# Every third PSUM copy of transposed p moves from ScalarE to VectorE, in the first batch

## The chip, the cores and the metric

The kernel runs on one core of one Trainium2 chip. Its engines, TensorE (PE, with its weight loads as PEld), VectorE (DVE), ScalarE (ACT), GpSimd (POOL) and SyncE (SP, which here issues the DMAs), each run their own list of instructions in order and wait for one another by semaphores. The metric is the device time of one execution in microseconds, the median of three runs.

## The reference

```python
def _attn_ref(q, k, v):                       # q, k, v: 4 x 8 x 1152 x 64, fp32
    q_pool = q.reshape(B, H, S // factor, factor, D).mean(axis=3)     # factor 2
    scores = scale * np.matmul(q_pool, k.transpose(0, 1, 3, 2))
    scores = scores - np.max(scores, axis=-1, keepdims=True)
    attn = np.exp(scores)
    attn = attn / (np.sum(attn, axis=-1, keepdims=True) + 1e-09)
    return np.matmul(attn, v).astype(np.float32)
...
    x = _moe_ref(x=x, **moe_kwargs)           # 512 -> 2048 -> 512, leaky relu
    return _moe2_ref(x=x, **moe2_kwargs)      # max of three 512 -> 768, then 768 -> 512
```

Attention over 4 batches of 8 heads, with each two rows of q averaged (576 queries against 1152 keys of 64), and behind it two MoE layers on the 2304 resulting rows.

## The kernel before

**Pairs and phases.** Heads are taken two at a time: 16 pairs, counted from 0, of which n = 0 to 3 are the first batch (NP = 4). The queries of a pair are worked in two phases: five tiles of 128 rows in the first (two of each head, and a fifth, `m`, of both), four in the second. A tile's scores are 128 x 1152 in three parts of 384. Nothing of the MoE layers can run until a batch's attention is through; from the second batch on MoE products and attention are interleaved, and TensorE always has MoE work to fill in. The first batch has none.

**A tile.** `scores` multiplies q by k (each split in two roundings) into three PSUM banks. In the first batch the outer two are a double bank, of which there are two (`s20`, `s21`), and the third is the single bank `s1`, used by every tile. VectorE takes the maximum of the double bank (L324, 128 x 768) and of the single one (L325, 128 x 384) and combines them (L326); ScalarE then takes the exponential of the single bank (L327), which frees it for the next tile's scores, and of the double one (L330). `normalise` (L348 to L354) makes the sums and, for the fifth tile, scales p.

**Transposes.** A phase has nine slots, one for each 128 keys. `probs_t` transposes that part of the phase's first four tiles on TensorE into one PSUM bank (`pst`, 128 x 512), and one copy (L377, on ScalarE) takes it to SBUF. Three such copies make a group (g = 0, 1, 2), `probs_m` adds the fifth tile's part for a group in a single copy (`psf`, L384, on VectorE), and `values` then multiplies the group with v into `pv`; `evac` takes the finished `pv` out (L422 to L424).

**What else uses the banks and the engines.** The pool `ps_m` has two banks in rotation, and everything else of the first batch goes through them: `psq` and `psk`, the transposes of q and k for the next pair, `pst`, `psf`, and `psr`, the sums. A bank is free again only when its copies are done: for `psq` scalings on ScalarE (L255), and their remainder on VectorE (L259); for `psk` two casts on ScalarE (L220) and two subtractions on VectorE (L223). The same engines also decode weights ahead of time: a load (L580), a scaling on ScalarE (L589) and a shift and a combination on VectorE (L592, L595), a rounding (L610), its remainder on GpSimd (L611), and a store (L619). Tiles of names `pspare`, `pend`, `kspare` and `qspare` are buffers lent by later parts.

**Order.** The program gives each slot its work in code, with preparation put at fixed slots. A scheduler then sets each engine's list, so an instruction's engine can change what stands near it. `EARLY` puts the maxima and exponentials ahead of work that the code issued some 300 instructions before them.

Of the kernel before, what the change touches and what calls it, by code (L numbers as in the profile page):

```python
# [22 lines left out]
def kernel(  # L23
# [21 lines left out]
    nc = tc.nc  # L45
    B, H, S, D = q.shape
    T = S // 2
    NP = H // 2
# [72 lines left out]
    def transpose(out, in_, eye):  # L121
        return on_pe(nc.tensor.transpose, out, in_, eye)
# [7 lines left out]
    def bank(name):  # L130
        turn[0] += 1
        pool = ps_w["m"] if ps_w and turn[0] % 2 == 0 else ps_m
        return pool.tile([128, 512], F32, tag="m", name=name)
# [154 lines left out]
    def keys_of(p, kt):  # L288
        c, k0 = divmod(kt * 128, SN)
        if c == 2:  # L290
            return p[1][:, k0:k0 + 128]
        return p[0].rearrange("p a b -> p (a b)")[:, kt * 128:(kt + 1) * 128]
# [75 lines left out]
    def probs_t(n, ph, kt):  # L368
        g = kt % PG
        if g == 0:  # L370
            pts[kt // PG] = pt_p.tile([128, PG, 2 * X0], F32, tag="pt", name="pt")
        w = (X0, T - X0)[ph]
        ps = bank("pst")
        for i in range(4):
            transpose(ps[:, i * 128:(i + 1) * 128], keys_of(ptl[n, ph, i], kt), ident)
        dst = pts[kt // PG][:, g, 0:2 * w].rearrange("p (j c) -> p j c", j=2)[:, :, 0:256]
        nc.scalar.copy(out=dst, in_=ps.rearrange("p (j c) -> p j c", j=2))  # L377

    def probs_m(n, gr):
        ps = bank("psf")  # L380
# [62 lines left out]
    def attention():  # L443
# [74 lines left out]
        for s in range(len(phases) * KT):  # L518
            n, ph = phases[s // KT]
            gr, g = divmod(s % KT, PG)  # L520
            done = 0
            want = CHAIN
            if s == 2 * NP * KT:
                done += yield from follow()
            probs_t(n, ph, gr * PG + g)
            done += TR * 4
            if g == PG - 1 and ph == 0:
                probs_m(n, gr)
                done += TR * PG
                want -= TR * PG  # L530
            c = now(s)
            if g == 0 and late:
                c += yield from follow()
            done += c
            yield done, max(0, want - c)
            yield 0, None
            if g == PG - 1:
                late.append((n, ph, gr))
# [133 lines left out]
    class Main:  # L672
        n = TM
# [11 lines left out]
    class Rest:  # L685
        n = TR_
# [102 lines left out]
    if True:  # L789
        nc.gpsimd.memset(ident, 0.0)  # L790
        nc.gpsimd.affine_select(
            out=ident, in_=ident, pattern=[[-1, 128]], compare_op=ALU.not_equal, fill=1.0, base=0, channel_multiplier=1
# [72 lines left out]
```

## Time and profile before

| what | value |
|---|---|
| median of 3 runs | 1360.38 us (1357.13 to 1360.44) |
| the profiled execution | 1356.42 us, of which its span 1354.7 us |
| TensorE busy | 1259.0 us, 93% |
| VectorE busy | 627.9 us, 46% |
| ScalarE busy | 633.5 us, 47% |
| GpSimd busy | 292.1 us, 22% |
| L377 copies of transposed p | 288, 167.4 us in all |
| first batch's attention | from about 33 us to 220 us |

The span is one profiled execution, seen from the first to the last instruction; 1.7 us of that execution lie outside. Busy shares are means over stages with different limits: the first fifth of the span, where the change lies, has gaps on every engine, and TensorE is nearly full behind it.

### The profile page before, as it was taken

How to read it: one execution, taken by the hardware profiler on the slowest of the kernel's cores; microseconds unless marked ns; L12 is line 12 of the kernel's file. 1: busy time of each engine (PE TensorE's matmuls, PEld its weight loads, DVE VectorE, ACT ScalarE, POOL GpSimd, SP SyncE). 2: the span in 40 equal slices, each digit the busy share in tenths (PEclk: the TensorE clock that was granted, in tenths of full speed). 3: DMA queues.
4: the chain of work that ended last, by engine and by line, in shares of the span. 5: the costliest groups of instructions: out<-in, count | busy, mean ns of one | idle time of the engine just before them, and what ended most of it. 6: DMA issues, size and time to landing. Idle time of an engine off the chain costs nothing.

```text
span 1354.7 us, 19162 instructions
## 1 busy us (share of the span) xinstructions
PE 1259.0 (93%) x7376; PEld 1015.6 (75%) x7376; DVE 627.9 (46%) x1106; ACT 633.5 (47%) x1253; POOL 292.1 (22%) x265
## 2 busy tenths in 40 slices
PE   5788878899898989999999989999999999999998
PEld 4556646677676877777787878787877788888888
DVE  5655554556656563455555454545464401222110
ACT  5767665666566664544444344545454422112111
POOL 1111022344454330121121010111110002224110
PEclk8888989999999999999999999999999999999999
DMA  5422053666767663444435344535343244333333
GB/s 158 123 74 57 18 149 118 215 210 209 248 202 229 208 188 131 132 136 131 154 126 157 123 128 163 149 109 150 128 141 116 95 154 154 129 126 124 108 126 109
DMA packets 86902, 193.29 MB, mean 143 GB/s; under 512 B 11292, under 2 KB 41756, under 8 KB 86812
## 3 DMA queue, kind: packets, MB, share of 16 engines
q1 hardware_dynamic: 86812, 192.08, 45.1%
q8 instruction: 58, 0.95, 0.3%
q14 instruction: 32, 0.26, 0.1%
HBM read 146.80 MB, written 35.13 MB: 134 GB/s over the span
## 4 chain that ended last, share of the span: by engine, by line
PE 75%; DMA 9%; DVE 7%; ACT 4%; issue 3%; POOL 2%; DVEq 0%; SPq 0%; ACTq 0%; POOLq 0%
PE m L108 41%; PE pv L108 10%; PE s L108 10%; PE pst L108 6%; PE o L108 6%; DMA wraw<-in_moe_w_out_dram 3%; DMA wraw<-in_moe_w_in_dram 2%; DMA wraw<-in_moe_w_dram 2%; DMA qraw<-in_q_dram 2%; DVE mx L334 1%; DVE wmant L595 1%; DVE mx L324 1%; ACT pt L377 1%; DVE q L259 1%; POOL wsplit L611 1%
## 5 line engine op out<-in xcount | busy, mean ns | idle before, releaser
L108 PE MATMUL m<-x,w 128*128 128x512 f32 x1224 | 308.9, 397 | 0.0
L108 PEld LDWEIGHTS m<-x,w 128*128 128x128 f32 x1224 | 222.7, 188 | 54.0 <-issue 12.8
L377 ACT COPY pt<-pst 128x512 f32<-128x512 f32 x288 | 167.4, 587 | 183.5 <-PE pst L108 182.3
L108 PE MATMUL s<-kt,q 128*128 128x384 f32 x840 | 190.6, 358 | 26.8 <-ACT p L335 14.1
L334 DVE TENSOR_REDUCE mx<-s 128x1 f32<-128x1152 f32 x108 | 146.4, 1355 | 116.2 <-PE s L108 114.9
L108 PEld LDWEIGHTS s<-kt,q 128*128 128x128 f32 x840 | 148.2, 195 | 39.2 <-ACT p L335 16.8
L108 PE MATMUL pst<-ident,p 128*128 128x128 f32 x1080 | 169.4, 277 | 8.4 <-ACT pt L377 3.5
L335 ACT ACTIVATE p<-s,mx 128x1152 f32<-128x1152 f32 x108 | 132.4, 1226 | 83.0 <-DVE mx L334 82.3
L108 PEld LDWEIGHTS pst<-ident,p 128*128 128x128 f32 x1080 | 131.6, 141 | 45.1 <-issue 11.6
L732 POOL TENSOR_TENSOR g<-t,g 128x512 fp32r<-128x512 f32 x64 | 84.5, 1322 | 369.7 <-DVE g L731 355.1
L108 PE MATMUL pv<-pt,v 128*64 128x320 f32 (+1 forms) x1008 | 149.9, 435 | 14.0 <-DVE pt L384 13.4
L108 PE MATMUL m<-g,w 128*128 128x512 f32 x576 | 149.8, 399 | 0.0
L108 PEld LDWEIGHTS m<-g,w 128*128 128x128 f32 x576 | 103.6, 188 | 24.5 <-issue 6.2
L108 PEld LDWEIGHTS pv<-pt,v 128*64 128x64 f32 x1008 | 67.8, 143 | 70.0 <-issue 20.5
L108 PE MATMUL m<-x,wsplit 128*128 128x512 f32 x408 | 108.5, 405 | 1.0 <-DVE kt L223 0.8
L730 ACT ACTIVATE t<-m 128x512 f32<-128x512 f32 x80 | 44.3, 555 | 128.2 <-PE m L108 128.2
L611 POOL TENSOR_TENSOR wsplit<-wmant,wsplit 128x512 fp32r<-128x512 f32 x56 | 74.1, 1327 | 92.8 <-ACT wsplit L610 71.0
L108 PEld LDWEIGHTS m<-x,wsplit 128*128 128x128 f32 x408 | 74.7, 191 | 20.5 <-issue 5.1
L731 DVE CAST g<-t 128x512 fp32r<-128x512 f32 x64 | 28.7, 448 | 111.2 <-ACT t L730 110.7
L760 DVE TENSOR_TENSOR t<-m,t 128x512 f32<-128x512 f32 (+1 forms) x60 | 38.2, 637 | 84.9 <-PE m L108 73.8
L670 POOL TENSOR_TENSOR y<-t,y 128x512 fp32r<-128x512 f32 x24 | 31.7, 1319 | 199.1 <-ACT y L669 199.1
L354 DVE TENSOR_SCALAR p<-p,sums 128x1152 f32<-128x1152 f32 x76 | 66.2, 870 | 2.7
(106 smaller groups left out, 1467.7 us busy)
## 6 DMA issues: line engine op xcount, KB each, us to landing
w<-w SPq DMA_DIRECT2D x168, 512.0 KB, 3.5
w<-wsplit SPq DMA_DIRECT2D x56, 512.0 KB, 5.1
wraw<-in_moe_w_out_dram SPq DMA_DIRECT2D x22, 512.0 KB, 4.1
wraw<-in_moe_w_dram SPq DMA_DIRECT2D x18, 512.0 KB, 4.0
qraw<-in_q_dram SPq DMA_DIRECT2D x15, 576.0 KB
kraw<-in_k_dram SPq DMA_DIRECT2D x15, 576.0 KB, 6.9
q<-q SPq DMA_DIRECT2D x52, 160.0 KB, 4.5
wraw<-in_moe_w_in_dram SPq DMA_DIRECT2D x16, 512.0 KB, 5.7
```

Source lines behind the costliest of these rows:

```text
L108: mm = f(*args, **kwargs)
L259: nc.vector.scalar_tensor_tensor(out=lo, in0=src, scalar=scale, in1=hi, op0=ALU.mult, op1=ALU.subtract)
L334: nc.vector.tensor_reduce(out=mx[:, 0:1], in_=ps[:, :, 0:SN], axis=AX.XY, op=ALU.max, negate=True)
L335: nc.scalar.activation(out=p[2], in_=ps[:, :, 0:SN], func=ACTF.Exp, bias=mx[:, 0:1], accum_out=rs[:, i:i + 1])
L354: nc.vector.tensor_scalar(out=x, in0=x, scalar1=rs[:, i:i + 1], scalar2=None, op0=ALU.mult)
L377: nc.scalar.copy(out=dst, in_=ps.rearrange("p (j c) -> p j c", j=2))
L611: nc.gpsimd.tensor_tensor(out=t[:, 1], in0=r, in1=t[:, 0], op=ALU.subtract)
L670: nc.gpsimd.tensor_tensor(out=t[:, 1], in0=src, in1=t[:, 0], op=ALU.subtract)
L730: nc.scalar.activation(out=t, in_=ps[:, 0:k.n], func=ACTF.Prelu, alpha=0.01)
L731: nc.vector.tensor_copy(out=gt[:, 0], in_=t)
L732: nc.gpsimd.tensor_tensor(out=gt[:, 1], in0=t, in1=gt[:, 0], op=ALU.subtract)
L760: nc.vector.tensor_tensor(out=t, in0=ps[:, 0:k.n], in1=t, op=ALU.max)
```

## The change

In the first batch the copy of the middle transposes of each group (g = 1; key parts 1, 4 and 7 of the nine) is issued on VectorE. That is 24 of the 288 copies. The bank, its size and its destination stay the same. Line numbers behind the edit are one higher in the changed kernel (L593 there is L592 here).

```diff
         dst = pts[kt // PG][:, g, 0:2 * w].rearrange("p (j c) -> p j c", j=2)[:, :, 0:256]
-        nc.scalar.copy(out=dst, in_=ps.rearrange("p (j c) -> p j c", j=2))
+        copy = nc.vector.tensor_copy if n < NP and g == 1 else nc.scalar.copy
+        copy(out=dst, in_=ps.rearrange("p (j c) -> p j c", j=2))
```

The scheduler puts other instructions of the first batch in a new order too; behind the first batch each engine's list is as it was, but for two neighbours on SyncE. Three places follow, as the difference of the lists (- before, + changed).

VectorE in the last group of pair 0's second phase; `mx_801` and `mx_832` are the maxima of the next phase's first two tiles, `pst_789` the middle transposes:

```order
 L324 TENSOR_REDUCE mx_801<-s20_117 128x1
 L325 TENSOR_REDUCE mx_801<-s1_119 128x1
+L378 COPY pt_767<-pst_789 128x512
 L324 TENSOR_REDUCE mx_832<-s21_118 128x1
 L326 TENSOR_REDUCE mx_801<-mx_801 128x1
```

The copy stands ahead of a second tile's maximum and of the combination for the first tile.

VectorE in the preparation of pair 3, in pair 1's second phase (`pst_1081` the middle transposes, `psk_1112` the first transposes of k):

```order
 L324 TENSOR_REDUCE mx_1099<-s20_117 128x1
+L378 COPY pt_1049<-pst_1081 128x512
 L325 TENSOR_REDUCE mx_1099<-s1_119 128x1
 L326 TENSOR_REDUCE mx_1099<-mx_1099 128x1
-L223 TENSOR_TENSOR kspare_317<-psk_1112,kspare_317 64x512 x2
 L348 TENSOR_TENSOR sums_941<-sums_941 128x5
 L349 TENSOR_SCALAR sums_941<-sums_941 128x5
 L350 RECIPROCAL sums_941<-sums_941 128x5
+L223 TENSOR_TENSOR kspare_317<-psk_1112,kspare_317 64x512 x2
```

The copy stands inside a tile's three maxima, and the subtractions for k have gone behind three steps on the sums. ScalarE at the same place:

```order
-L377 COPY pt_1049<-pst_1081 128x512
 L364 COPY rb256_122<-psr_1108 128x256
-L220 CAST kspare_317<-psk_1112 64x512 x2
+L220 CAST kspare_317<-psk_1112 64x512
 L327 ACTIVATE pend_1043,sums_941<-s1_119,mx_1099 128x384
 L330 ACTIVATE pspare_1100,sums_941<-s20_117,mx_1099 128x768
-L377 COPY pt_1049<-pst_1121 128x512
+L220 CAST kspare_317<-psk_1112 64x512
+L378 COPY pt_1049<-pst_1121 128x512
```

Between the two casts of k there now stands a tile's exponential.

VectorE at the end of pair 3's first phase (`wraw_2012` and `wraw_2075` are two weight loads one after the other, `pst_1684` the middle transposes, `mx_1751` the maximum of a tile of the next phase):

```order
-L595 SCALAR_TENSOR_TENSOR wmant_1940<-wraw_1938 128x512
+L596 SCALAR_TENSOR_TENSOR wmant_1940<-wraw_1938 128x512
+L596 SCALAR_TENSOR_TENSOR wmant_1950<-wraw_1948 128x512
 L223 TENSOR_TENSOR kt0_1642<-psk_1669,kt0_1642 64x512 x2
-L595 SCALAR_TENSOR_TENSOR wmant_1950<-wraw_1948 128x512
+L593 TENSOR_SCALAR wraw_2012<-wraw_2012 128x512
+L378 COPY pt_1662<-pst_1684 128x2x256
 L334 TENSOR_REDUCE mx_1751<-s_1741 128x1
```

The decode of `wraw_2012`, which waits for its load, has come ahead of the copy and of a maximum. A few instructions later on the same engine:

```order
-L592 TENSOR_SCALAR wraw_2012<-wraw_2012 128x512
-L384 COPY pt_1662<-psf_1714 128x6x64
-L595 SCALAR_TENSOR_TENSOR wmant_1978<-wraw_1976 128x512
+L593 TENSOR_SCALAR wraw_2075<-wraw_2075 128x512
+L385 COPY pt_1662<-psf_1714 128x6x64
+L596 SCALAR_TENSOR_TENSOR wmant_1978<-wraw_1976 128x512
 L223 TENSOR_TENSOR kt1_1643<-psk_1719,kt1_1643 64x512 x2
-L592 TENSOR_SCALAR wraw_2075<-wraw_2075 128x512
```

The decode of `wraw_2075` has come ahead of the fifth tile's copy. Its load has moved on SyncE, ahead of the load of the next batch's q:

```order
+L620 DMA w1_132<-wsplit_1934 128x1024
+L581 DMA wraw_2075<-in_moe_w_out_dram 128x4x256
 L171 DMA qraw_1838<-in_q_dram 72x2x1024
-L580 DMA wraw_2075<-in_moe_w_out_dram 128x4x256
-L264 DMA q10_125<-q10_125 64x640
```

The load follows directly on a store of split weights now.

## Rows read from the trace of the kernel before

**Rows 1.** Windows: each engine's busy us (instructions), clock, DMA share, GB/s.
```profile
33.00:185.00 152.00, 122.32 (x772) 88.29 (x773) 87.97 (x192) 106.00 (x251) 19.47 (x22) 0.93 0.24 63
...
220.00:1354.00 1134.00, 1091.26 (x6373) 894.57 (x6372) 503.77 (x848) 488.62 (x923) 260.06 (x218) 0.99 0.48 152
```

**Rows 2.** The chain that ended last, 33 to 185 us, by line.
```profile
by line: PE pv L108 20.0%; PE s L108 17.7%; PE pst L108 10.2%; DVE mx L324 7.9%; ACT pt L377 4.3%; issue 3.4%; DVE mx L325 2.9%; DVE kspare L223 2.9%; DMA wraw<-in_moe_w_in_dram 2.6%; ACT pspare L330 2.3%; DMA wraw<-in_moe_w_out_dram 2.3%; 
```

**Rows 3.** Waits of PE, 33 to 185 us: total us, times, longest.
```profile
PE psk L108 <- ACT pt L377: 4.0, 2, 2.3
PE pst L108 <- ACT pt L377: 3.5, 6, 1.6
```

**Rows 4.** Groups by form, DVE 33:220, ACT 33:185: busy, mean ns | idle before, releaser.
```profile
L324 DVE TENSOR_REDUCE mx<-s 128x1 f32<-128x768 f32 x31 | 29.6, 955 | 30.8 <-PE s L108 30.4
L325 DVE TENSOR_REDUCE mx<-s 128x1 f32<-128x384 f32 x31 | 17.1, 552 | 11.3 <-PE s L108 11.2
...
L384 DVE COPY pt<-psf 128x384 f32<-128x384 f32 x12 | 6.6, 549 | 0.0
...
L377 ACT COPY pt<-pst 128x512 f32<-128x512 f32 x61 | 35.5, 587 | 28.5 <-PE pst L108 28.3
```

**Rows 5.** Timeline by engine, 85 to 90 us: start, length, instruction, idle before.
```profile
86.27 0.95 DVE L324 TENSOR_REDUCE mx<-s 128x1 f32<-128x768 f32 x1
87.25 0.15 DVE L326 TENSOR_REDUCE mx<-mx 128x1 f32<-128x2 f32 x1
...
86.41 1.07 ACT L377 COPY pt<-pst 128x512 f32<-128x512 f32 x2 [4.40 <-PE pst L108]
...
88.16 0.62 PE L108 MATMUL s<-kspare,qspare 128*128 128x384 f32 x2 [0.45 <-ACT p L327]
```

**Rows 6.** Timeline by engine, 112 to 126.5 us.
```profile
116.25 0.96 DVE L324 TENSOR_REDUCE mx<-s 128x1 f32<-128x768 f32 x1
...
115.91 0.59 ACT L377 COPY pt<-pst 128x512 f32<-128x512 f32 x1 [0.16 <-PE pst L108]
...
116.63 0.60 PE L108 MATMUL psk<-ident,kraw 128*128 128x128 f32 x4
...
120.01 0.44 PE L108 MATMUL psq<-ident,qraw 72*128 72x72 f32 x4 [2.10 <-DVE kspare L223]
...
122.95 1.12 PE L108 MATMUL psk<-ident,kraw 128*128 128x128 f32 x4 [1.74 <-ACT pt L377]
```

**Rows 7.** Timeline by engine, five other places between 46 and 168 us.
```profile
46.24 0.56 DVE L325 TENSOR_REDUCE mx<-s 128x1 f32<-128x384 f32 x1 [1.26 <-PE s L108]
...
46.13 3.47 PE L108 MATMUL pv<-pt,v 128*64 128x320 f32 x12
...
62.69 0.62 PE L108 MATMUL s<-kspare,qspare 128*128 128x384 f32 x2 [1.12 <-ACT p L327]
...
79.69 1.12 PE L108 MATMUL psk<-ident,kraw 128*128 128x128 f32 x4 [2.28 <-ACT pt L377]
...
131.88 0.62 PE L108 MATMUL s<-kt,q 128*128 128x384 f32 x2 [0.40 <-ACT p L327]
...
167.44 0.62 PE L108 MATMUL s<-kspare,qspare 128*128 128x384 f32 x2 [1.83 <-ACT p L327]
```

**Rows 8.** Timeline by engine, 180 to 206 us.
```profile
185.26 0.37 SPq L580 DMA_DIRECT2D wraw<-in_moe_w_out_dram  x1
...
189.56 1.36 DVE L334 TENSOR_REDUCE mx<-s 128x1 f32<-128x1152 f32 x1 [1.53 <-PE s L108]
...
193.25 0.55 DVE L384 COPY pt<-psf 128x384 f32<-128x384 f32 x1
...
200.04 0.43 DVE L592 TENSOR_SCALAR wraw<-wraw 128x512 int32<-128x512 uint32 x1 [3.91 <-DMA wraw<-in_moe_w_out_dram]
...
201.04 0.65 PE L108 MATMUL pv<-pt,vx 128*64 128x256 f32 x4 [0.71 <-DVE xf L422]
```

**Rows 9.** Line L580, the weight loads: issue to landing.
```profile
DMA to landing us min/median/max: 3.6/4.1/6.0
```

## Prediction

> **What bounds the kernel now.** I first set two stretches side by side [rows 1]. From 220 us to the end TensorE is busy for 1091.26 of 1134 us, 96%, and nothing of the change is there, so whatever time the change wins or loses before 220 us is carried to the end as it is. In the first batch (33 to 185 us) no engine is full: of 152 us TensorE works 122.32, ScalarE 106.00, VectorE 87.97. TensorE runs its instructions in order and so does every other engine, so this stretch is bound by who hands on late to whom, not by a sum of work. The chain of that stretch [rows 2] and TensorE's waits in it [rows 3] say what ScalarE's copies cost now: the copies of transposed p are 4.3% of the chain, 6.5 us of 152, and TensorE waits on them 4.0 us ahead of the transposes of k and 3.5 us ahead of the next transposes of p. The largest item that is not TensorE is VectorE's double-bank maximum, 7.9% or 12 us. That is the engine the change loads.
>
> **Prices.** A ScalarE copy of 128x512 out of PSUM takes 587 ns; VectorE's nearest row is the same kind of copy at 128x384, 549 ns [rows 4]. VectorE's maxima over 384 and 768 elements differ by 403 ns [rows 4], 1.05 ns an element, so 128 more elements make about 549 + 134 = 683 ns, an estimate; it cannot be under 549, and 955 ns for 768 elements bounds it above. I take 0.68. Of 288 copies 24 move (4 pairs, 2 phases, 3 groups, one of three): ScalarE loses 24 x 0.587 = 14.1 us and VectorE gains 24 x 0.68 = 16.3 us, so 2.2 us of engine time is added in all, and neither becomes full (VectorE about 104 of 152). The difference of 0.1 us a copy in favour of ScalarE shows in these rows. [...]
>
> **Where the copy is free.** Before its double-bank maxima VectorE stands idle 30.8 us in 31 instances, all but 0.4 of it waiting for the scores [rows 4], about 1 us each. In 13 of the 24 places the moved copy stands in such a gap of 0.8 us or more, and its transposes are done before the gap opens. There I put its cost at nothing; were that cover gone, each would cost its 0.68 us, 8.8 in all. I also put the gain there at nothing, since TensorE had not been waiting for the ScalarE copy at those places. Three more lie behind 200 us.
>
> **Where it is not free.** The order of the changed kernel puts the copy in front of the maximum on which an exponential, and then the next scores, hang. I followed the clock of the old trace through the new order, place by place:
>
> Pair 0 (pairs counted from 0), second phase, last group [rows 5]. The copy comes between the two double-bank maxima. In the old trace the second starts at 86.27 and the combining step (L326) at 87.25, whence the exponential and the scores at 88.16. The copy's transposes are done when ScalarE copies at 86.41; with 0.68 of copy ahead, L326 starts at 87.93 and, with what lies between L326 and the scores as before (0.91), the scores go from 88.16 to 88.9 or 89.1: up to +0.95, which I take.
>
> Preparation of pair 3 [rows 6], middle group of pair 1's second phase. The copy stood on ScalarE at 115.91, and freed the bank for the transposes of k at 116.63. On VectorE it comes behind the maximum at 116.25 to 117.2, ends at 117.9, and the transposes of k start at 117.97, +1.3. Then the two roundings of k on ScalarE have both parts of an exponential between them (L327 and L330 by the order), so the second half of k is subtracted later: the next transposes of q go from 120.01 to 122.05, and those of k from 122.95 to 125.15: +2.2. The same pattern in the preparation of pair 2 ends at the transposes of k of 79.69 [rows 7], with a stall there of 2.28 us that ScalarE's other work sets, so I count +0.7.
>
> Others, all to TensorE rows of the same group. At 46.13 (pair 0's first group) the products with v: the copy of the fifth tile's transposes now stands behind the maximum that started at 46.24 and took 0.56, so it ends no sooner than 46.80 + 0.55, and the products start at 47.4 to 48.0: +1.5. At 62.69 (that phase's last group) the scores waited for an exponential; ahead of its maximum there now stand the moved copy's part that exceeds VectorE's wait for a weight (0.3), the fifth tile's copy (0.55) and a weight decode of 0.4: +1.3. At 167.44 (pair 2's last group) the scores waited 1.83 us for an exponential whose maxima have one copy more ahead and the two scalings of p between them: +0.9. At 131.88 (pair 1's last group) the combining step has been moved ahead of the copy and of a maximum of 0.95, with ScalarE's own queue holding most of that: -0.35.
>
> The end of the batch, 183 to 220 us [rows 8]. Here waits for weights have moved. The decode of the load issued at 185.26 now stands ahead of the copy and the wide maximum that began at 189.56. Such a load lands 3.6 to 6.0 us after its issue, 4.1 the median [rows 9], so 188.9 to 191.3. With decode and copy (0.43 + 0.68) ahead the maximum slips by 0.4 to 2.9, and by 0.9 at the median. The decode of the next load stands ahead of the copy of 193.25. That load is now issued sooner, behind a store and ahead of the load of q; I estimate that it has landed by 193 to 195, which costs nothing to 2 us. Against it, the old trace has VectorE blocked 3.91 us until 200.04 by this same load, and TensorE waiting 0.71 us at 201.04 for what was queued behind it; with the load there sooner about 1 us is returned. I take +1.0 for the maximum, +1.0 for the copy of 193.25 and -1.0 for this: +1.0 for the whole stretch, between 0 and +5.
>
> **Sum.** 0.95 + 2.2 + 0.7 + 1.5 + 1.3 + 0.9 - 0.35 + 1.0 = +8.2 us. The profiled execution took 1356.42 us, so it would take 1364.6. That execution lies 4.0 us under the median of the runs (1360.38) and close to the lowest (1357.13), so by the median the sum gives 1368.6. I take 1366.0, between the two, which puts the kernel before at 1357.8 on the same scale. Of the terms, the preparation of pair 3 and the first product are the largest, and all of them scale with the price of the copy and with how long VectorE's queue holds it.
>
> **Rivals.** *No change*, 1360.4: a late step on TensorE shortens the stall that follows it, and the 30.8 us of VectorE's idle time take more than I allowed; half of the seven terms ahead of 183 us vanish (3.6 us left) and the load that goes out earlier makes the last one -1.0, +2.6 in all. For it: the stretch has 30 us of TensorE idle to be filled. Against it: the stalls that I used are already the ones that end last at their places. [...]
>
> *Faster*, 1354.5: of the 7.5 us that TensorE waits ahead of transposes for ScalarE's copies, 6.5 by the chain [rows 2, 3], about half comes back, most of it where k and q are prepared and ScalarE has casts, scalings, exponentials and copies in one queue, and the maxima lose nothing: -3.3. It decides at one place: if VectorE reaches the copy of 115.91 before 116.5, the bank of k comes free sooner than before and the term of +2.2 turns into a gain. Against it stands VectorE's maximum from 116.25 to 117.2 in front of it.
>
> *Much slower*, 1370.5 or more: at 193.25 the copy waits behind a weight that lands only at 197 to 199, as the old trace has it noticed at 200.04; then the end of the batch costs +5 or +6 in place of +1.
>
> **How the numbers follow.** A measurement of this kernel tells about 0.3% from no change, 4.1 us: under 1356.3 is faster, over 1364.5 slower. My forecast of a few us lost has 0.46, much slower 0.12, no change 0.27, faster 0.15. That gives slower 0.58, same 0.27, faster 0.15. The range goes from 1357 (0.14 below, nearly all of the faster case) to 1373 (0.05 above, the tail where both late weights are paid in full); it takes in VectorE's copy at 549 ns (24 copies shorter by 0.13, under 2 us on the path) and at 0.95.
>
> **What would show it.** VectorE's new rows of 128x512 at 0.64 to 0.70 us. The first MoE products, which end the batch's stretch, 6 to 10 us later, and the rest of the program as long as it was. In the preparation of pair 3 a wait of TensorE for the copy by VectorE ahead of k. TensorE's waits for ScalarE's copies of p nearly gone, and those for VectorE's copies and for the first exponential (L327) grown by more. I would be wrong if the start of that MoE work stands where it stood, or earlier: then the stalls have absorbed what VectorE's queue adds; or if what is lost is lost behind 220 us, in which nothing has moved.

## The result and the profile after

The changed kernel takes 1368.11 us (median of 4 runs, 1366.07 to 1370.28) against 1359.69 of the kernel before in the same comparison (4 runs, 1357.13 to 1360.44): ratio 1.0065, 95% interval 1.0042 to 1.0088. It is slower, by 8.4 us or 5.7 to 12.0 by the interval, where I had said +8.2 and 1366.0. The profiled execution has a span of 1366.6 us (1354.7 before).

The windows of the changed kernel, that answer to [rows 1]:

```profile
33.00:185.00 152.00, 121.26 (x752) 88.18 (x751) 95.50 (x202) 90.29 (x216) 15.60 (x19) 0.90 0.23 61
...
220.00:1354.00 1134.00, 1094.74 (x6360) 894.51 (x6360) 516.49 (x855) 491.81 (x924) 261.01 (x219) 0.99 0.48 152
```

In 152 us of the first batch ScalarE works 15.7 us less and VectorE 7.5 us more. TensorE gets through fewer instructions in the same stretch, 752 for 772, though an engine is relieved. The groups by form, VectorE from 33 to 220 us, answer to [rows 4]:

```profile
L324 DVE TENSOR_REDUCE mx<-s 128x1 f32<-128x768 f32 x31 | 29.6, 954 | 7.5 <-PE s L108 6.7
...
L378 DVE COPY pt<-pst 128x512 f32<-128x512 f32 x23 | 15.9, 690 | 17.5 <-PE pst L108 17.0
```

A copy takes 690 ns (680 to 693 over all 24), as estimated. The idle time ahead of the double-bank maxima fell from 30.8 to 7.5 us: the copies do stand there. TensorE's waits from 33 to 185 us, against [rows 3] and these three rows of the kernel before:

```profile
PE s L108 <- ACT p L327: 7.5, 7, 1.8
...
PE psq L108 <- ACT pt L377: 2.2, 3, 1.2
...
PE pst L108 <- DVE kspare L223: 1.7, 1, 1.7
```

In the changed kernel:

```profile
PE s L108 <- ACT p L327: 9.0, 6, 2.1
PE psq L108 <- ACT pt L378: 6.3, 3, 2.9
PE pst L108 <- DVE kspare L223: 4.6, 2, 4.3
PE psk L108 <- ACT pt L378: 2.7, 2, 1.4
PE pst L108 <- ACT pt L378: 2.5, 3, 1.8
...
PE psk L108 <- DVE pt L378: 2.1, 2, 1.1
```

Ahead of k and p the waits for ScalarE's copies went from 7.5 to 5.2 us. But those ahead of the transposes of q, 2.2 us before, are 6.3, and 2.1 us for VectorE's copies are new. The longest single wait, 4.3 us for VectorE's subtractions of k, stands at the first moved copy. In the preparation of pair 3 both stand, against [rows 6] (TensorE's timeline):

```profile
124.46 0.66 PE L108 MATMUL psk<-ident,kraw 128*128 128x128 f32 x4 [1.07 <-DVE pt L378]
128.45 0.74 PE L108 MATMUL psq<-ident,qraw 72*128 72x72 f32 x4 [2.90 <-ACT pt L378]
...
131.79 1.11 PE L108 MATMUL psk<-ident,kraw 128*128 128x128 f32 x4 [1.38 <-ACT pt L378]
```

What came into this place late by 6.60 us leaves it late by 8.84, at 131.79 for 122.95.

**Reading the loss as stairs.** Up to 220 us nearly the same instructions run in both kernels, so the start of an exponential in one trace less its start in the other shows where time is lost, except where the exponential itself has another place in ScalarE's list. The table gives these differences against the first profile of before, for both profiles of the changed kernel and a second one of before. The last line is the start of the first MoE products (218.58 us in the first profile).

| us before | before again | changed | changed again | place just passed |
|---|---|---|---|---|
| 37.48 | +0.70 | +0.35 | +0.38 | nothing moved yet |
| 57.78 | +0.67 | +0.86 | +0.86 | pair 0's first group |
| 75.78 | +2.00 | +3.36 | +0.28 | its last group, start of the preparation of pair 2 |
| 99.17 | +2.11 | +6.60 | +3.49 | rest of that preparation, last group of the second phase |
| 114.20 | +2.08 | +6.59 | +3.48 | two copies in gaps |
| 133.89 | +2.16 | +8.05 | +4.93 | preparation of pair 3 |
| 161.05 | +2.17 | +8.05 | +4.92 | five copies in gaps |
| 166.72 | +2.16 | +8.37 | +5.24 | pair 2's last group |
| 178.49 | +2.17 | +8.37 | +5.24 | two copies in gaps |
| 218.58 | +2.37 | +9.95 | +6.94 | end of the batch, moved decodes |

Some stairs are steps of the kernel: 1.45 us at the preparation of pair 3 and 1.6 to 1.7 at the end in both profiles, nothing over nine copies in VectorE's gaps. Others are a matter of the run. Before the first moved copy a run may be late by 0.7, and between 57 and 76 us the two profiles of one kernel differ by 3 us. One profile of this stretch is good to some 3 us, and behind it two of one kernel differ by up to 5.7: from the first MoE products to the end of the span it is 1136.1 and 1141.8 us in the two profiles of before, 1138.1 and 1134.5 in the changed kernel's. There the change shows nothing, and the medians carry the verdict.

### The profile page after: what moved, and what is told of

The parts are those of the page before. It is cut to its first block, busy times and chain, and to the rows that moved or that the text cites. A ratio compares the mean times of both kernels' runs of the same rounds, so it can differ in the third digit from the quotient of the medians.

```text
span 1366.6 us, 19163 instructions
## 1 busy us (share of the span) xinstructions
PE 1265.8 (93%) x7376; PEld 1021.1 (75%) x7376; DVE 650.6 (48%) x1130; ACT 622.2 (46%) x1229; POOL 290.8 (21%) x265
## 4 chain that ended last, share of the span: by engine, by line
PE 78%; DVE 8%; DMA 6%; ACT 4%; issue 3%; POOL 1%; DVEq 0%; ACTq 0%; POOLq 0%; SPq 0%
PE m L108 42%; PE pv L108 11%; PE s L108 10%; PE pst L108 7%; PE o L108 5%; DMA wraw<-in_moe_w_out_dram 3%; DVE mx L334 2%; DVE mx L324 1%; DMA qraw<-in_q_dram 1%; DVE wmant L596 1%; DMA wraw<-in_moe_w_in_dram 1%; DVE pt L385 1%; ACT q L255 1%; ACT pt L378 1%; PE psq L108 1%
## 5 line engine op out<-in xcount | busy, mean ns | idle before, releaser
L378 ACT COPY pt<-pst 128x512 f32<-128x512 f32 x264 | 153.6, 586 | 178.2 <-PE pst L108 177.3
L108 PE MATMUL pv<-pt,v 128*64 128x320 f32 (+1 forms) x1008 | 153.2, 443 | 14.9 <-DVE pt L385 14.0
L205 POOL TENSOR_TENSOR qraw<-qraw 72x512 f32<-72x512 f32 (+1 forms) x32 | 40.5, 1285 | 125.7 <-DMA qraw<-in_q_dram 111.1
```

Source lines behind the costliest of these rows:

```text
L108: mm = f(*args, **kwargs)
L205: engine.tensor_tensor(out=a[1 - e], in0=a[0], in1=a[1], op=ALU.add)
```

## The experiments

All but three runs choose the copies that move by another condition in the line `copy = nc.vector.tensor_copy if ... else nc.scalar.copy`, so for each only the condition is shown. "Costly" are the eight places that the prediction priced one by one. Each variant's first MoE products are told against the 218.58 and 220.95 of the two profiles of before. In several of them the scheduler orders some work behind 222 us otherwise too, so a span alone is not told as a result.

**The 16 copies in gaps.**

```diff
+if n < NP and g == 1 and (n, ph, kt) not in ((0, 0, 1), (0, 0, 7), (0, 1, 4),
+    (0, 1, 7), (1, 1, 4), (1, 1, 7), (2, 1, 7), (3, 0, 7))
```

> VectorE makes 16 of the 24 copies: the 13 that stand in its idle time ahead of a maximum and the 3 behind 200 us; the other 8 stay on ScalarE. Measured against the kernel before at the first MoE products (218.58 us before, 228.53 with all 24). Theory (a copy costs only where it stands ahead of a maximum or a subtraction that TensorE waits for): 218.6, at most 0.7 later, and the median within 2 us of before. Rival (each copy that goes to VectorE costs the same, by its longer duration and its queue): 16 of 24 parts of 9.95, so 225.2 and 6 us in the median.

1359.84 us against 1357.59 (10 and 13 runs): ratio 1.0009, interval 0.9992 to 1.0027, no difference. The median is 2.25 us higher, a little over the 2 that I allowed, and the first MoE products come at 222.33, later than allowed too. But the stairs lie at 43.7 (1.0), 62 (1.4), 87 (0.4) and 173 us (1.6), in every case where other kernels without a copy there have them as well; 1.2 came back between 118 and 131, and nothing was lost at the copies between 90 and 114 or at the end. But for the 16 copies, every engine's list in the trace reads as in the kernel before. The groups by form show the gaps as filled as in the changed kernel:

```profile
L324 DVE TENSOR_REDUCE mx<-s 128x1 f32<-128x768 f32 x31 | 29.6, 955 | 7.7 <-PE s L108 6.6
...
L378 DVE COPY pt<-pst 128x512 f32<-128x512 f32 x16 | 11.0, 690 | 16.0 <-PE pst L108 15.8
```

So 11 us more of work on VectorE cost nothing that the runs tell; the interval leaves room for up to 3.7 us.

**The 8 costly copies.**

```diff
+if (n, ph, kt) in ((0, 0, 1), (0, 0, 7), (0, 1, 4), (0, 1, 7),
+    (1, 1, 4), (1, 1, 7), (2, 1, 7), (3, 0, 7))
```

> The other 8 copies alone go to VectorE, those that I priced one by one. Theory: the whole of the loss, first MoE products at 228 to 229 and a median 8 to 10 us above before. Rival (the same cost for each copy): 8 of 24 parts of 9.95, 221.9 and 3 us in the median.

1366.78 us against 1357.59: ratio 1.0082, interval 1.0050 to 1.0114, and first MoE products at 229.49. A third of the copies, with the new order that the scheduler gives the lists around them, makes the whole loss. The same cost for each copy is out. Copy and order are not separated here.

**One copy alone, preparation of pair 3.**

```diff
+if (n, ph, kt) == (1, 1, 4)
```

> One copy alone goes to VectorE, the middle one of pair 1's second phase, in the preparation of pair 3; the list of weight decodes at 183 us changes with it as in the changed kernel. Theory: the transposes of k of 122.95 come 2.2 us later, at 125.1 to 125.3, with everything ahead unmoved, and the decodes add 1 to 2, so the first MoE products at 221.8 to 222.5. Rival (the loss in the changed kernel came from what was late already when it got there): under 0.8 at 122.95 and the first MoE products before 220.5.

Late by 1.11 at 114.20 and by 2.83 at 133.89: 1.7 in this place. Its TensorE rows:

```profile
118.97 0.66 PE L108 MATMUL psk<-ident,kraw 128*128 128x128 f32 x4 [1.05 <-DVE pt L378]
122.97 0.57 PE L108 MATMUL psq<-ident,qraw 72*128 72x72 f32 x4 [2.90 <-ACT pt L378]
...
126.14 1.12 PE L108 MATMUL psk<-ident,kraw 128*128 128x128 f32 x4 [1.22 <-ACT pt L378]
```

They are the waits of the changed kernel to 0.2 us, with nothing late ahead but the 1.11: 126.14 less 122.95 less 1.11 is 2.1, where I had said 2.2. The last step, first MoE products at 223.89, is later than the 222.5 allowed, since a group of products at 171 us ran at 2.83 us for 1.52; the end of the batch took 0.5.

**One copy alone, last group of pair 0's first phase.**

```diff
+if (n, ph, kt) == (0, 0, 7)
```

> One copy alone, the middle one of the last group of pair 0's first phase; the weight decodes at 183 us change with it too. In the changed kernel this place lost 3.9 us where I had 1.3. Theory A (the queue costs 1.3 to 1.9, and the longer stall of TensorE is followed by a stretch at the lower clock, in which the 12 products with v take 3.4 us in place of 1.84): 3 to 4 us at the transposes of q of 67.48, and products of 3 us or more. Theory B (the surplus came from being late already by 0.6): 1.3 us and products of 1.84.

Theory A in its mechanism, neither in size: the transposes of q come at 70.27, 2.3 us late beyond the 0.47 that the run had before. Here are the scores and the products behind them, first in this kernel, then in the one with only the copy of pair 1 moved, where this place is as before:

```profile
63.89 0.62 PE L108 MATMUL s<-kspare,qspare 128*128 128x384 f32 x2 [2.03 <-ACT p L327]
64.44 3.27 PE L108 MATMUL pv<-pt,v 128*64 128x320 f32 x12
```

```profile
63.76 0.62 PE L108 MATMUL s<-kspare,qspare 128*128 128x384 f32 x2 [1.02 <-ACT p L327]
64.31 1.83 PE L108 MATMUL pv<-pt,v 128*64 128x320 f32 x12
```

The stall is 1.0 us longer and the products behind it take 3.27 us for 1.83. The windows over these products give the granted clock (the third number from the end): 0.54 of full in this kernel and 1.00 in the other. In the first profile of before, 56 of the 384 half microseconds from 33 to 225 us stand at 0.50 and 317 at 1.00, so 0.54 is near the lower of the two.

```profile
64.44:67.60 3.16, 3.16 (x13) 1.17 (x12) 0.71 (x2) 1.83 (x6) 0.00 (x0) 0.54 0.02 5
```

```profile
64.31:66.10 1.79, 1.79 (x14) 0.80 (x13) 0.71 (x2) 1.66 (x6) 0.00 (x0) 1.00 0.00 0
```

And at 75.78 only 0.6 us are left (+0.47 before, +1.08 behind). ScalarE's list gives time back here: it now has all four scalings of `psq` and the cast behind them ahead of the exponential of 68.65, where the kernel before has two scalings and the cast behind it. So VectorE's part of that work waits less, first before, then here:

```profile
71.22 1.53 DVE L259 SCALAR_TENSOR_TENSOR q<-psq,q 64x160 fp32r<-64x160 f32 x4 [3.14 <-ACT kt L220]
```

```profile
72.72 1.57 DVE L259 SCALAR_TENSOR_TENSOR q<-psq,q 64x160 fp32r<-64x160 f32 x4 [1.36 <-ACT kt L220]
```

From the transposes of q (67.48 before, 70.27 here) to this step it is 3.74 us before and 2.45 here, 1.3 less. The clock does not follow the copy in every run: the changed kernel has these products at 3.46 us in its first profile and at 1.84 in its second, with the same copy ahead. First MoE products at 223.59.

**Before and changed, each once more.** No edit.

> The kernel before, unchanged, profiled once more. In three variants, places that no copy had been moved at are 1.0 us late at 43.7, 1.3 to 1.6 late at the products with v of 56 or 173, and 0.4 to 1.2 early at 131, against the first profile. Theory (the clock that TensorE is granted after a stall differs from run to run, so a profile of the first batch is good to some 2 us): the same jumps turn up here, each group of 12 products with v at one of two durations, and the first MoE products at 219 to 222.5. Rival (the jumps are the variants' own): 218.6 within 0.4 and every group as it was.

> The changed kernel, profiled once more. Theory: the places where a moved copy stands ahead of a maximum or a subtraction lose what they lost (1.2 at the transposes of k of 116.63, 1.8 at those of q of 120.01), and the number of groups of products with v at the long duration may differ; first MoE products at 227 to 231. Rival (what was lost was a chance of that run): some of these places lose nothing, first MoE products under 226.

First MoE products at 220.95 in the one and 225.52 in the other. Their times are 1364.47 us for the kernel before, above its 13 other runs of that comparison (1353.80 to 1362.08, median 1356.62), and 1361.78 for the changed one, inside them: two single runs tell nothing of the change. For the kernel before the jumps turned up again: late by 0.7 at 37 us, by 1.0 more at 43.7, of which 1.1 came back at 54; the products of 56 us at 2.96 us for 1.84. The last two are the clock, as the theory has it (the products of 46 us took 2.44 for 3.47, at 0.74 for 0.50; those of 56 us had 0.59 for 1.00). The first two are not. At 25 us TensorE waited for GpSimd's averaging of q, which had waited for its load, and ScalarE's scaling of these transposes came at 25.65 for 24.91. And the 1.0 is a scaling of p on VectorE (L354) that took 1.62 us for 0.62; it takes 1.58 to 1.72 in the six profiles in which that averaging begins before it or up to 0.04 us behind it, and 0.62 in the seven in which it begins 0.06 us or more behind. For the changed kernel the wait for VectorE's copy ahead of k and the stair of 1.45 at the preparation of pair 3 were there again, but the surplus between 57 and 76 was not, and 225.52 is under the 226 that I had given the rival. So the rival is right for that one place and wrong for the rest. Its loss is not all chance, though. The products of 63 us took 3.46, 1.84, 3.11 and 3.27 us in the four profiles of kernels with the copy of pair 0's last first-phase group moved (the changed one twice, the 8 costly copies, this copy alone), and 1.83 or 1.84 in all the others. Those of 56 us took 2.7 us or more in eight of 13 profiles, with moved copies and without.

**Pair 3's six copies alone.**

```diff
+if n == 3 and g == 1
```

> Only pair 3's six copies go to VectorE (174 to 220 us), and here the weight decodes and loads stay where they were in the order. Theory (at the end of the batch the decodes that come ahead of copy and maximum make the loss): the first MoE products no later than pair 3's start is, within 0.4. Rival (the copies themselves load VectorE's queue there): 1 to 1.6 us lost between 179 and 218.

+2.27 at 178.49 and +2.62 at 218.29 by the exponentials: 0.35. The copies without the moved decodes cost next to nothing. The other kernels agree: where VectorE's decodes keep their place the end takes 0.20 (before again), 0.04 (the 16 copies), 0.35 (this one, with one of ScalarE's scalings and a load of k moved) and -0.86 (the last of the three below, with two of ScalarE's scalings moved). Where they are moved it takes 0.47, 1.62, 1.05, 1.18 and 1.49, in kernels that leave pair 3's copies on ScalarE, and 1.4 to 1.7 with them.

**Two other copies.**

```diff
+if (n, ph, kt) in ((0, 1, 6), (1, 1, 6))
```

> Two other copies go to VectorE, and all middle ones stay on ScalarE: those for which TensorE waits 2.28 us at 79.69 and 1.74 at 122.95 ahead of transposes of k. Theory (a copy pays on VectorE where ScalarE's queue is the late one): the transposes of k of 79.69 come 1.0 us sooner and those of 122.95 0.4 sooner, in all -1.4, with +0.5 to +1.6 at the end from the decodes that this order moves too; the median within 2 us of before. Rival (VectorE's subtractions for q, pushed back by 0.69, are late in turn): no gain at either, up to 1.4 lost.

1362.89 us against 1356.62: ratio 1.0040, interval 1.0024 to 1.0057, slower; a miss. The waits ahead of k did shrink, 2.28 to 0.91 at the one and 1.74 to 1.34 at the other:

```profile
79.18 1.12 PE L108 MATMUL psk<-ident,kraw 128*128 128x128 f32 x4 [0.91 <-DVE pt L378]
...
87.06 0.15 DVE L326 TENSOR_REDUCE mx<-mx 128x1 f32<-128x2 f32 x1
...
87.94 0.59 ACT L378 COPY pt<-pst 128x512 f32<-128x512 f32 x1 [0.31 <-PE pst L108]
...
88.43 0.59 ACT L327 ACTIVATE p<-s,mx 128x384 f32<-128x384 f32 x1
...
89.16 0.62 PE L108 MATMUL s<-kspare,qspare 128*128 128x384 f32 x2 [1.30 <-ACT p L327]
```

The transposes of k come 1.38 us sooner than the run's lateness of 0.87 would have them. At the scores of 88.16 it is given back, 0.85 of it in a wait of 1.30 for 0.45. The order says why: ScalarE's list has the copy of the next phase's first transposes (`pst_820`, at 87.94) ahead of the exponential here, where the kernel before has it two places behind. VectorE's combining step is done at 87.21, and the exponential starts at 88.43. 2.0 us late at the end of the batch against the first profile of before, of which 1.05 from the decodes, and not late against the second. What makes the other 4 us of the median, behind 222 us, these runs do not tell; between 236 and 300 us its lists of TensorE and ScalarE differ from the kernel before, which no other variant's do.

**Three copies, each alone.** The conditions are, in this order:

```diff
+if (n, ph, kt) == (0, 0, 1)
+if (n, ph, kt) == (0, 1, 4)
+if (n, ph, kt) == (0, 1, 7)
```

> One copy alone, the middle one of pair 0's first group (I had +1.5 for it; with the start of a run as uneven as the two profiles of before show, the changed kernel had something between -0.2 and +0.8). Theory A (the place costs what I said): the exponential of 47.02 and the groups of products behind it 1.2 to 1.5 later than in the later of the two profiles of before. Theory B (it costs nothing, since the copy stands ahead of a maximum that waits for scores anyway): within 0.4 of one of the two. At the end of the batch the moved decodes: +0.5 to +1.6 between 179 and 218.

> One copy alone, the middle one of the preparation of pair 2. With the next one it lost 2.4 to 2.7 between 75.78 and 87.44 where I had 0.7 + 0.95. Theory A (this place is as the preparation of pair 3, so the missing part is here): 1.4 to 1.9. Theory B (0.7 as I said): 0.5 to 0.9. The decodes are moved here as well: +0.5 to +1.6 between 179 and 218.

> One copy alone, the middle one of the last group of pair 0's second phase, which comes between two double-bank maxima; the decodes stay where they were. Theory: 0.95 between 75.78 and 87.44 as I said (0.8 to 1.1) and nothing at the end, within 0.4 between 179 and 218. Rival: 0.1 to 0.4 there, with the larger part in the preparation ahead of it.

First group: +1.89 at 47.02, against +1.75 in the second profile of before, so theory B as it was put. But that profile had come to 43.70 late by 1.75, and this one by 1.19. With that taken off, the products start 1.55 us later than before, which is theory A's place and size:

```profile
48.13 0.56 DVE L385 COPY pt<-psf 128x384 f32<-128x384 f32 x1
...
48.87 2.59 PE L108 MATMUL pv<-pt,v 128*64 128x320 f32 x12
```

The other three profiles with this copy have the same 1.55 or 1.56 there; no profile without it starts them later. Behind it 0.9 comes back, since these products took 2.59 us for 3.47 (granted clock 0.70 for 0.50). From 43.70 to 54.73 the four profiles lose 0.23 to 1.40 us, while the nine without the copy lose nothing or win up to 1.07. The preparation of pair 2: 0.70 from 68.65 to 75.78 and 0.22 more by 87.44, where kernels without this copy have 0 to 0.5: theory B, some 0.7. But the casts and subtractions of k keep their places in this kernel, while the changed kernel moves them here as in the preparation of pair 3. Last group of the second phase: 1.5 from 75.78 to 87.44, which is 1.0 to 1.5 beyond kernels with nothing moved there, and 0.44 more by 99.17, outside of both; and at the end it wins 0.86, where I had said within 0.4. In this kernel `pst_820` has been moved ahead of the exponential too:

```profile
88.63 0.15 DVE L326 TENSOR_REDUCE mx<-mx 128x1 f32<-128x2 f32 x1
...
89.04 0.59 ACT L378 COPY pt<-pst 128x512 f32<-128x512 f32 x1 [0.80 <-PE pst L108]
89.52 0.59 ACT L327 ACTIVATE p<-s,mx 128x384 f32<-128x384 f32 x1
...
90.25 0.62 PE L108 MATMUL s<-kspare,qspare 128*128 128x384 f32 x2 [1.30 <-ACT p L327]
```

From the first double-bank maximum (84.93 before) to the combining step this run loses 0.59 us, the moved copy's part, and from there to the exponential 0.70 more, that of `pst_820`. The wait of 1.30 is that of the kernel with two other copies, in which the middle copy here had stayed on ScalarE, and of the changed kernel, where the two parts are 0.59 and 0.20 (0.59 and 0.20 again in its second profile). All five kernels with `pst_820` ahead of the exponential (the changed one, the 8 costly copies, the two other copies, the last group of pair 0's first phase, and this one) lose some 0.44 us between 89.60 and 99.17; those without it lose nothing there.

**The 16 copies, each made twice.**

```diff
         copy(out=dst, in_=ps.rearrange("p (j c) -> p j c", j=2))
+        if copy is not nc.scalar.copy:
+            copy(out=dst, in_=ps.rearrange("p (j c) -> p j c", j=2))
```

> As the kernel with only the 16 copies in VectorE's idle time, but each of the 16 is made twice, the second time over the first. In the single form VectorE's idle time ahead of the double-bank maxima fell from 30.8 to 7.7 us and in 8 of the 13 places nothing of it was left. Theory (a copy is free for as long as it fits in that time): the second copy costs 0.6 in those 8 places and 0.1 in five, some 5 us, so 5 us above the single form at 179 and 0.3 to 0.5% in the median. Rival (VectorE is not what counts at those places): under 1.5 us at 179 and no difference in the median.

1396.17 us against 1356.00, ratio 1.0296 (1.0257 to 1.0336), but the edit is not what the expectation says: the condition is true for every copy, so that ScalarE's 272 are made twice as well, in all batches. The median says nothing on the question. Two of its wait rows, from 33 to 185 us, do say something:

```profile
PE pst L108 <- DVE pt L380: 4.1, 5, 1.0
...
PE psf L108 <- DVE pt L380: 2.6, 4, 1.0
```

TensorE waits 6.7 us for VectorE's second copies (L380) and waited for none of the single ones in the kernel with 16. That fits gaps that hold one copy and not two; it is no measure of it, since ScalarE's doubled copies moved all the rest.

## Why the prediction was right

**The verdict and the size.** Loss against before at the first MoE products, both profiles of each kernel averaged: (9.95 + 6.94 - 0 - 2.37) / 2 = 7.3 us, and with the 8 costly copies, which repeat the changed kernel's list at those places, 10.91 against the first profile of before and 8.54 against the second. I had said 8.2. The medians give 8.4. That the cost lies in eight places and that the other copies are free is shown by the two kernels that split them, 1.0009 and 1.0082. That the sum meets the medians to 0.2 us is luck in part: single pairs of profiles give 4.6 to 9.95, and some terms were too large, others too small.

**Term by term.** Net is what a place takes beyond kernels that have nothing moved there.

| term | said | net, measured |
|---|---|---|
| first products with v | +1.5 | 1.55 at the products; 0.2 to 1.4 left by 54.73 |
| last group, pair 0's first phase | +1.3 | 0.7 at the scores of 62.69; 0.6 by 75.78 with the products at 0.54 of the full clock (alone) |
| preparation of pair 2 | +0.7 | 0.7 (alone, in another order than the changed kernel's) |
| last group, second phase | +0.95 | 1.0 to 1.5, and 0.4 behind (alone); 0.8 and 0.4 in the changed kernel |
| preparation of pair 3, and pair 1's last group | +1.85 | 1.45 together, 1.7 without the second |
| pair 2's last group | +0.9 | 0.32 |
| end of the batch | +1.0 | 1.4 to 1.7 |

The preparation of pair 3 came out as worked: 2.1 us at the transposes of k with this copy alone, 2.24 in the changed kernel, where I had 2.2. By the exponentials 1.45 to 1.7 of it is left; kernels with nothing moved there won up to 1.2 in the same stretch, so net it may be more. The delay of the first products came as worked too, and so did its cause, the fifth tile's copy behind VectorE's maximum. What I did not have is the clock: in the four profiles with this copy these products ran at 0.59 to 0.81 of full, where the first profile of before had 0.50, and that gave 0.4 to 1.2 us back.

The last group of pair 0's first phase was mis-sized: half of the 1.3 stood at the scores, the clock could add to it, and ScalarE's new order behind it gave back 1.3. In the changed kernel's second profile, with these products at 1.84 us, the whole stretch from 57.78 to 75.78 wins 0.57, the start of the preparation of pair 2 included. In the last group of the second phase I looked at VectorE's list alone. Its copy does delay the combining step, by 0.59 where I had 0.68; but on ScalarE a copy of transposes that come later has moved ahead of the exponential, and adds 0.2 to 0.7 there and some 0.44 behind. The wait for the scores is the same 1.30 for 0.45 when the middle copy is not moved at all.

**The end of the batch.** The mechanism was as said: decodes that wait for weights stand ahead of copy and maximum. VectorE's timeline of the changed kernel, against [rows 8]:

```profile
199.30 0.43 DVE L593 TENSOR_SCALAR wraw<-wraw 128x512 int32<-128x512 uint32 x1 [3.63 <-DMA wraw<-in_moe_w_out_dram]
199.76 0.69 DVE L378 COPY pt<-pst 128x512 f32<-128x512 f32 x1
200.37 1.35 DVE L334 TENSOR_REDUCE mx<-s 128x1 f32<-128x1152 f32 x1
...
203.88 0.52 DVE L593 TENSOR_SCALAR wraw<-wraw 128x512 int32<-128x512 uint32 x1 [0.32 <-DMA wraw<-in_moe_w_out_dram]
204.32 0.54 DVE L385 COPY pt<-psf 128x384 f32<-128x384 f32 x1
```

With 8.37 us of lateness taken off, the maximum slips by 2.4 (I said 0.9, up to 2.9) and the fifth tile's copy by 2.7 (up to 2); the weight that had blocked VectorE for 3.91 us now blocks it for 0.32, and part comes back behind it: the exponential of 192.14 is 3.9 us later than at the stretch's start, the first MoE products 1.6. That the decodes do this and not pair 3's copies is shown by the kernels with either: 0.47 to 1.62 us with moved decodes alone, 0.35 with the copies alone.

**What was said of the waits.** The copies' 690 ns, the wait for VectorE's copy ahead of k and the growth behind the first exponential (7.5 to 9.0 us) came. That TensorE's waits for ScalarE's copies would be nearly gone did not: with those ahead of q they went from 9.7 to 11.5 us, because ScalarE's copies of the same group now stand behind exponentials or casts that wait for VectorE. The rival *faster* had the same view of them, and it fails for that reason.

**What stays open.** The surplus of the changed kernel's first profile between 57 and 76 us is two groups of products at a lower granted clock (2.72 us at 0.66 from 57.42 us and 3.46 at 0.52 from 66.16, where the first profile of before has 1.84 at 1.00 for both); which runs get the one at 56 us, and why one of four escaped the one at 63, no experiment here settles. In the eight places the copy and the scheduler's other moves come together; of the copies run alone, only that of the preparation of pair 2 (0.7 us) had the lists of VectorE and ScalarE around it in the old order. How much of a doubled copy the gaps would have held was not measured.

## What to carry to other kernels

Of an operation that moves to a less busy engine, ask at each place what stands behind it in that engine's list and whom that releases: 16 copies, 13 of which filled idle time ahead of a maximum, were free, and 8 that stood in front of one, with the new order around them, cost the whole 8 us. Read the new order on every engine, for steps that the scheduler moved along with the copy cost time here (a cast behind an exponential, a later copy ahead of one, a decode that waits for a load: 1.6 to 1.7 us at the end of the batch alone), and at one place gave 1.3 us back. And where single profiles of one kernel differ by several us, compare by stairs between neighbouring points and leave the verdict to medians.

## What the runs showed of the hardware

A group of 12 products with v runs at either of two durations in the first batch, whatever the kernel: 1.52 or 2.83 us at 256 columns, 1.84 or 3.47 at 320, with some between. The groups of 81 and 124 us had the long one (2.5 to 2.83) in every run, behind stalls of 0.9 to 2.3 us; that of 56 us had 1.84 in one profile of before and 2.96 in the other, granted clock 1.00 and 0.59:

```profile
56.00:57.80 1.80, 1.80 (x14) 0.80 (x13) 1.68 (x7) 1.80 (x6) 0.00 (x0) 1.00 0.69 198
```

```profile
57.00:59.90 2.90, 2.90 (x13) 1.21 (x12) 2.09 (x8) 2.90 (x7) 0.40 (x1) 0.59 0.58 180
```

I had expected two profiles of one kernel to be alike at that scale. A wait that a change lengthens by 1 us can so be followed by 1.4 us that the wait itself does not show, as at 63 us in three of four profiles. It also goes the other way: products that started 1.55 us later at 46 us took 2.24 to 3.06 us, where seven of the nine profiles without that copy had 3.40 to 3.47.

And the clock is not the only thing that differs from run to run. The same scaling on VectorE at 40 us took 0.62 us or 1.58 to 1.72, and in all 13 profiles it was the long one exactly where GpSimd's averaging of q had begun, or began within 0.04 us.
